# Half of the SiLU products split into float32r, one shared buffer pool, and an accumulating DMA in the rational stage

## The chip, the cores and the metric

One program on one core of a Trainium2 chip. The metric is the device time of one execution in microseconds. The engines named below are TensorE (PE in the profile, its weight loads PEld), VectorE (DVE), ScalarE (ACT), GpSimd (POOL) and the DMA queue of SyncE (SP). Each engine runs its own instructions strictly in the order in which the program lists them; semaphores make one engine wait for another.

## The reference

Three stages over 12480 tokens of 128 channels, all in float32; the second and third have 2048 hidden units.

```python
a2k = softmax(agents @ k.T / sqrt(128));  agent_v = a2k @ v      # 49 agents
x   = softmax(q @ agents.T / sqrt(128)) @ agent_v
h   = x @ moe_w_in;   x = (h * sigmoid(h)) @ moe_w_out           # SiLU
h   = x @ moe2_w_in                                              # rational function
P   = a[0] + a[1]*h + a[2]*h**2 + a[3]*h**3
Q   = 1 + abs(b[0])*abs(h) + abs(b[1])*h**2
out = (P / (Q + 1e-6)) @ moe2_w_out
```

The four weight matrices arrive as float64 and are turned into float32 on the chip.

## The kernel before

The tokens are cut into 25 groups: 24 of 512 tokens and one of 192. The 2048 hidden units are cut into 8 *pairs* of 2 x 128, so the work tile of one pair is 128 x 1024 float32 (4 KB in each partition). For each group, with p from 0 to 7:

- **M1** (lines 537, 538): 4 matmuls of pair p in float32r into a PSUM tile h; **S1** (line 544): ScalarE, s = Silu(h).
- **M2** (line 551): s times w_out in plain float32, summed over the pairs in the one PSUM bank x2. The profile lists each float32 matmul as two records, so a pair has 4.
- **XS** (lines 564, 565): VectorE splits x2 into a float32r high part xh and a rest xl.
- **M3** (lines 574 to 576): x2 times w2_in as three float32r products, low weights x xh, high weights x xl, high weights x xh: 6 matmuls for each pair, into a tile h.
- **U** (line 585 on VectorE for pairs 0 to 3, line 583 on ScalarE for pairs 4 to 7), **W1** (line 610), **W2** (line 614), both on VectorE: the cubic by Horner's rule without a[0], in a tile z.
- **AB** (line 592, ScalarE): m = |h|. **N** (line 598) and **Q** (line 606), both on GpSimd: y = (|b1| m + |b0|) m.
- **L** (line 619) and **R** (line 622), ScalarE, on two pairs at once (128 x 2048): 1/(1+y+1e-6) as sigmoid(-ln(y + 1e-6)).
- **G2** (line 626, VectorE): z = (z + a0) y. **M4** (line 635): z times w2_out in plain float32 into the PSUM bank ot. **O1** (line 647, ScalarE copy), **O2** (line 655, transposes), **O3** (line 661, ScalarE copy, and the store on SP).

Once for two groups the q stage makes the softmax weights of 1024 tokens: QT, QTc (line 459, ScalarE copy, which also issues the next q load on SP), QS, QV, QX, QM, QE, QN, QB, QBc (line 516, two ScalarE copies), QBl. Before the groups, k, v and the weights are loaded, the agents' attention is formed, and 16 jobs convert the weights: C0 to C2 on VectorE and ScalarE, C3 (line 756, GpSimd), and for w2_in also C4 (line 760, ScalarE) and C5 (line 764, GpSimd), which split it into float32r parts.

PSUM has three h tiles of two banks, one x2 and one ot bank. SBUF tiles come from rings of their own: 5 for s, 13 for z, 2 for m, 6 of 8 KB for y. The order of all instructions is written by a planner, `scheduled`, that plays the program through with a table of costs (`COST`), picks by priorities (`PLACE`), and emits the steps in its order. Silu, Ln, Sigmoid and Exp each need their own table on ScalarE, so the planner runs all L of a group, then all R, and S1 outside of that. Its first L of a group waits, in the plan, until `READY_Y` denominators are done (4 halves before, so all eight pairs).

Of the kernel before, what the change touches and what calls it, by code (L numbers as in the profile page):

```python
# [996 lines left out]
```

## Time and profile before

| | |
|---|---|
| three timed runs | 1263.23, 1265.34, 1265.42 us; median 1265.34 us |
| span of the profiled execution, first to last instruction | 1261.5 us, 3.8 us under that median |
| PE busy | 1235.0 us, 98% of the span |
| ACT busy | 1076.0 us, 85% |
| DVE busy | 1003.4 us, 80% |
| POOL busy | 764.2 us, 61% |
| DMA | HBM read 27.59 MB, most of it in the first 60 us |

The profiled execution is known by its span; what lies around the span is taken as the 3.8 us to the median. A busy PE is a PE with some matmul in it; the busy time alone doesn't say that it runs at its peak.

### The profile page before, as it was taken

The numbers are of one execution on the slowest core, as the hardware profiler recorded it, in microseconds if no ns is written. First come the engines' busy times: TensorE is split into PE (matmuls) and PEld (weight loads), VectorE is DVE, ScalarE is ACT, GpSimd is POOL, SyncE is SP. The second block draws the span as 40 slices with busy tenths as digits, with TensorE's granted clock in tenths as the row PEclk, the third lists the DMA queues.
The fourth block names the chain that finished last, engine by engine and source line by source line (L and its number), as shares of the span: only waits on it lengthen the run. The fifth ranks groups of instructions, "written<-read, shape, count | busy, mean of one in ns | idle before, by whom it ended". The sixth has DMA issues, their size and how long they took to land.

```text
span 1261.5 us, 12078 instructions
## 1 busy us (share of the span) xinstructions
PE 1235.0 (98%) x4393; PEld 740.7 (59%) x4393; DVE 1003.4 (80%) x960; ACT 1076.0 (85%) x997; POOL 764.2 (61%) x434
## 2 busy tenths in 40 slices
PE   9899899999999999999999999999999999999987
PEld 5656465556556556556566565565555565555654
DVE  4977887888868869869869869769769769769895
ACT  7677988988988988988988978978978979978896
POOL 2248667666566656656655755755755755755863
PEclk9999999999999999999999999999999999999999
DMA  9820000000000000000000000000000000000000
...
DMA packets 14675, 34.75 MB, mean 28 GB/s; under 512 B 1575, under 2 KB 5720, under 8 KB 14616
## 3 DMA queue, kind: packets, MB, share of 16 engines
...
q8 instruction: 35, 0.57, 0.2%
...
HBM read 27.59 MB, written 6.39 MB: 27 GB/s over the span
## 4 chain that ended last, share of the span: by engine, by line
PE 86%; DVE 6%; ACT 4%; DMA 2%; issue 1%; POOL 0%; SPq 0%; POOLq 0%; ACTq 0%; DVEq 0%
PE x L551 25%; PE ot L635 23%; PE h L537 7%; PE h L574 7%; PE h L538 7%; PE h L576 7%; PE h L575 7%; DVE z L610 2%; DVE z L614 1%; DVE z L585 1%; PE h L468 1%; PE h L451 1%; DMA kv<-in_k_dram 1%; PE ot L655 1%; DVE z L626 1%
## 5 line engine op out<-in xcount | busy, mean ns | idle before, releaser
L598 POOL TENSOR_SCALAR y<-m,bab 128x1024 f32<-128x1024 f32 (+1 forms) x200 | 265.4, 1329 | 409.8 <-ACT m L592 402.9
L606 POOL TENSOR_TENSOR y<-y,m 128x1024 f32<-128x1024 f32 (+1 forms) x200 | 469.0, 2357 | 7.5
L551 PE MATMUL x<-s,wo 128*128 128x512 f32 (+1 forms) x800 | 358.9, 584 | 3.1 <-ACT s L544 2.8
L635 PE MATMUL ot<-z,w2o 128*128 128x512 f32 x768 | 349.8, 596 | 6.8 <-DVE z L626 4.6
L610 DVE TENSOR_TENSOR z<-z,h 128x1024 f32<-128x1024 f32 (+1 forms) x200 | 237.8, 1191 | 141.2 <-ACT z L583 134.1
L626 DVE SCALAR_TENSOR_TENSOR z<-z,a_sb,y 128x1024 f32<-128x1024 f32 (+1 forms) x200 | 264.6, 1372 | 4.7 <-ACT y L622 4.7
L592 ACT ACTIVATE m<-h 128x1024 f32<-128x1024 f32 (+1 forms) x200 | 197.1, 1000 | 81.2 <-PE h L576 72.9
L614 DVE SCALAR_TENSOR_TENSOR z<-z,a_sb,h 128x1024 f32<-128x1024 f32 (+1 forms) x200 | 249.9, 1252 | 5.0 <-ACT m L592 0.5
L544 ACT ACTIVATE s<-h 128x1024 f32<-128x1024 f32 (+1 forms) x200 | 193.3, 1005 | 59.5 <-PE h L538 59.1
L635 PEld LDWEIGHTS ot<-z,w2o 128*128 128x128 f32 x768 | 143.6, 190 | 162.2 <-issue 145.1
L551 PEld LDWEIGHTS x<-s,wo 128*128 128x128 f32 x800 | 147.7, 190 | 138.5 <-issue 127.0
L574 PE MATMUL h<-xh,w2l 128*128 128x512 f32 (+1 forms) x400 | 190.9, 477 | 1.6 <-DVE z L614 1.2
L619 ACT ACTIVATE y<-y,eps 128x2048 f32<-128x2048 f32 (+1 forms) x100 | 191.4, 1957 | 0.8 <-POOL y L606 0.5
L537 PE MATMUL h<-xt,w1a 128*128 128x512 f32 (+1 forms) x400 | 185.9, 466 | 0.8 <-DVE z L614 0.7
L622 ACT ACTIVATE y<-y 128x2048 f32<-128x2048 f32 (+1 forms) x100 | 185.0, 1878 | 0.3
L576 PE MATMUL h<-xh,w2h 128*128 128x512 f32 (+1 forms) x400 | 155.9, 390 | 0.0
L575 PE MATMUL h<-xl,w2h 128*128 128x512 f32 (+1 forms) x400 | 155.3, 388 | 0.0
L538 PE MATMUL h<-xt,w1b 128*128 128x512 f32 (+1 forms) x400 | 155.1, 389 | 0.0
L585 DVE TENSOR_SCALAR z<-h,a_sb 128x1024 f32<-128x1024 f32 (+1 forms) x100 | 130.8, 1312 | 5.7 <-PE h L576 3.8
L583 ACT ACTIVATE z<-h,a_sb 128x1024 f32<-128x1024 f32 (+1 forms) x100 | 118.3, 1184 | 5.5 <-PE ot L635 3.5
L537 PEld LDWEIGHTS h<-xt,w1a 128*128 128x128 f32 x400 | 75.6, 189 | 44.1 <-issue 16.0
L574 PEld LDWEIGHTS h<-xh,w2l 128*128 128x128 f32 x400 | 75.9, 190 | 36.7 <-issue 20.0
...
## 6 DMA issues: line engine op xcount, KB each, us to landing
q<-in_q_dram SPq DMA_DIRECT2D x12, 512.0 KB, 3.3
out_dram<-ob SPq DMA_DIRECT2D x24, 256.0 KB, 2.0
raw<-in_moe_w_in_dram SPq DMA_DIRECT2D x8, 512.0 KB, 4.9
raw<-in_moe_w_out_dram SPq DMA_DIRECT2D x8, 512.0 KB, 7.5
s<-in_k_dram SPq DMA_DIRECT2D x7, 512.0 KB, 7.4
kv<-in_v_dram SPq DMA_DIRECT2D x7, 512.0 KB, 7.7
kv<-in_k_dram SPq DMA_DIRECT2D x5, 512.0 KB, 10.3
s<-in_v_dram SPq DMA_DIRECT2D x5, 512.0 KB, 8.0
```

What stands on the lines that cost most here:

```text
L537: nc.tensor.matmul(h[:, c, :w], w1a[:, f], xt, start=True, stop=False)
L538: nc.tensor.matmul(h[:, c, :w], w1b[:, f], xt, start=False, stop=True)
L551: nc.tensor.matmul(x2_t[i][:, : cols(i)], wo[:, 2 * p + c, :], s[:, c, : cols(i)], start=(p == 0 and c == 0), stop=(p == NP - 1 and c == 1),)
L574: nc.tensor.matmul(h[:, c, :w], w2l[:, f], xh_t[i], start=True, stop=False)
L575: nc.tensor.matmul(h[:, c, :w], w2h[:, f], xl_t[i], start=False, stop=False)
L576: nc.tensor.matmul(h[:, c, :w], w2h[:, f], xh_t[i], start=False, stop=True)
L598: nc.gpsimd.tensor_scalar(out=y_t[i, p // 2][:, p % 2], in0=m_t[i, p], scalar1=bab[:, 1:2], scalar2=bab[:, 0:1], op0=ALU.mult, op1=ALU.add,)
L606: eng.tensor_mul(out=y, in0=y, in1=m_t.pop((i, p)))
L610: nc.vector.tensor_mul(out=z, in0=z, in1=h)
L614: nc.vector.scalar_tensor_tensor(out=z, in0=z, scalar=a_sb[:, 1:2], in1=h, op0=ALU.add, op1=ALU.mult)
L626: nc.vector.scalar_tensor_tensor(out=z, in0=z, scalar=a_sb[:, 0:1], in1=r, op0=ALU.add, op1=ALU.mult)
L635: nc.tensor.matmul(ot_t[i][:, : cols(i)], w2o[:, 2 * p + c, :], z[:, c, :], start=(p == 0 and c == 0), stop=(p == NP - 1 and c == 1),)
```

## The change

1. **M2 split for half of the pairs.** Pairs 2, 3, 6 and 7 (`SPLIT = [1, 3]`) get what M3 has: SH (VectorE copy of s to float32r), SL (GpSimd subtraction; in group 0 VectorE for pairs 2 and 6), then six float32r matmuls. Pairs 0, 1, 4, 5 stay as they are. Two more weight jobs need C4 and C5.
2. **The rational stage is rescaled.** A once-run step CF (33 small VectorE instructions on 128 x 1 columns, 2 on ScalarE) forms coefficients, so that x2 can be multiplied by |b0| in XS, and the denominator becomes 1 + |h| + kap h². SQ (ScalarE, Square with a per-partition scale) gives kap h² for all 8 pairs; W1 becomes a scalar_tensor_tensor of h and that square; U, N and Q are gone.
3. **|h| is added by DMA.** Y issues, on GpSimd's queue, an SBUF to SBUF DMA of 512 KB with accumulation, m into y. L and R now work on one pair each.
4. **Copies moved.** QTc, QBc, O1 and O3 go from ScalarE to VectorE.
5. **One pool of 34 slots of 4 KB** for s, sh, sl, xh/xl, y, m, z, q, qT and the output tiles, in place of the rings. q loads (LQ) and stores (OD) are steps of their own on SP's queue. The loads have a new order, and group 0 no longer waits for all weight jobs before AB.
6. The planner's costs and priorities are new; `READY_Y` is 8.

The core of the diff:

```diff
-U_ACT = (4, 5, 6, 7)
-NZ = 13
-NY = 6
-NM = 2
-NS = 5
+SPLIT = [1, 3]
+HIGH = 'DDDDDDDD'
+LOW = "PPPPPPPP"
+LOW_0 = "DPDPDPDP"
+POLY = 'SSSSSSSS'
+ABS = "AAAAAAAA"
+MAG = 'GGGGGGGG'
+COPY = 'DDDD'
+NF = 34
...
+    def SH(i, p, slot):
+        sh = t_f(slot, F32R)
...
+            (eng.dma_start if HIGH[p] == "G" else eng.tensor_copy)(sh[:, :, :w], s_t[i, p][:, :, :w])
+    def SL(i, p, slot):
...
+        eng = nc.gpsimd if (LOW if i else LOW_0)[p] == "P" else nc.vector
+        eng.tensor_sub(
+            out=sl[:, :, :w], in0=s_t.pop((i, p))[:, :, :w], in1=sh_t[i, p][:, :, :w].bitcast(F32)
+        )
...
+            if p // 2 in SPLIT:
...
+                nc.tensor.matmul(x2, low, sh, start=start, stop=False)
+                nc.tensor.matmul(x2, high, sl, start=False, stop=False)
+                nc.tensor.matmul(x2, high, sh, start=False, stop=stop)
...
+        nc.vector.tensor_scalar_mul(out=xh, in0=ps[:, :w], scalar1=B0)
+        nc.vector.scalar_tensor_tensor(
+            out=xl, in0=ps[:, :w], scalar=B0, in1=xh.bitcast(F32), op0=ALU.mult, op1=ALU.subtract
+        )
...
+    def SQ(i, p, slot):
+        y = part_of(y_t, i, p, slot)
+        nc.scalar.activation(y, h2_t[i, p][:, :, : cols(i)], AF.Square, scale=ROOT)
...
+            nc.vector.scalar_tensor_tensor(
+                out=part_of(z_t, i, p, slot), in0=h, scalar=COEF[2], in1=y_t[i, p],
+                op0=ALU.mult, op1=ALU.add,
+            )
...
+    def Y(i, p, slot=None):
+        m = m_t.pop((i, p))
+        y = y_t[i, p]
+        if MAG[p] == "G":
+            nc.gpsimd.dma_start(out=y, in_=m, accum_op=ALU.add)
...
+    def L(i, p):
+        nc.scalar.activation(y_t[i, p], y_t[i, p], AF.Ln, bias=eps)
+    def R(i, p):
+        nc.scalar.activation(y_t[i, p], y_t[i, p], AF.Sigmoid, scale=-1.0)
...
+                done = sum((done_y(h), g, h) in end for h in range(8))
                 if batch is None and (p or done < READY_Y):
                     return None
```

## Rows read from the trace of the kernel before

**Rows 1.** Busy time by stretch: us; PE, PEld, DVE, ACT, POOL; clock; DMA share; GB/s

```profile
20.00:40.00 20.00, 16.98 (x103) 9.70 (x103) 14.41 (x29) 17.20 (x35) 3.65 (x3) 0.91 0.96 350
60.00:200.00 140.00, 131.84 (x435) 78.07 (x436) 114.83 (x123) 114.98 (x114) 89.43 (x51) 0.99 0.08 25
608.35:704.17 95.82, 95.82 (x318) 56.76 (x317) 76.11 (x68) 83.62 (x73) 58.71 (x32) 1.00 0.03 11
1150.00:1261.50 111.50, 99.55 (x380) 62.28 (x378) 87.91 (x90) 90.17 (x91) 69.64 (x43) 0.98 0.03 11
```

**Rows 2.** Waits, 608.35 to 704.17 us: who waited for whom, us, times, longest

```profile
ACT m L592 <- PE h L576: 7.2, 6, 3.8
...
ACT s L544 <- PE h L538: 4.2, 4, 1.8
```

**Rows 3.** Timeline of PE: start, us, line, tiles, count

```profile
620.55 3.60 PE L551 MATMUL x<-s,wo 128*128 128x512 f32 x8
623.98 0.60 PE L655 MATMUL ot<-ident,oT 128*128 128x128 f32 x4
...
632.34 0.40 PE L574 MATMUL h<-xh,w2l 128*128 128x512 f32 x1
...
635.14 0.40 PE L537 MATMUL h<-xt,w1a 128*128 128x512 f32 x1
```

**Rows 4.** Timeline of ACT

```profile
606.52 1.19 ACT L583 ACTIVATE z<-h,a_sb 128x1024 f32<-128x1024 f32 x1
607.61 1.01 ACT L592 ACTIVATE m<-h 128x1024 f32<-128x1024 f32 x1
608.51 2.00 ACT L619 ACTIVATE y<-y,eps 128x2048 f32<-128x2048 f32 x1
...
621.94 0.58 ACT L647 COPY oT<-ot 128x512 f32<-128x512 f32 x1
622.41 3.73 ACT L622 ACTIVATE y<-y 128x2048 f32<-128x2048 f32 x2
```

**Rows 5.** Groups by line and shape, whole span, ACT: busy us, mean ns

```profile
L619 ACT ACTIVATE y<-y,eps 128x2048 f32<-128x2048 f32 x96 | 187.9, 2000 | 0.3
...
L622 ACT ACTIVATE y<-y 128x2048 f32<-128x2048 f32 x96 | 181.9, 1922 | 0.3
...
L619 ACT ACTIVATE y<-y,eps 128x768 f32<-128x768 f32 x4 | 3.5, 928 | 0.5 <-POOL y L606 0.5
L622 ACT ACTIVATE y<-y 128x768 f32<-128x768 f32 x4 | 3.2, 835 | 0.0
```

**Rows 6.** Groups by line and shape, 608.35 to 704.17 us, DVE

```profile
L610 DVE TENSOR_TENSOR z<-z,h 128x1024 f32<-128x1024 f32 x17 | 20.7, 1218 | 15.0 <-ACT z L583 14.9
L614 DVE SCALAR_TENSOR_TENSOR z<-z,a_sb,h 128x1024 f32<-128x1024 f32 x16 | 20.5, 1279 | 0.4
L585 DVE TENSOR_SCALAR z<-h,a_sb 128x1024 f32<-128x1024 f32 x8 | 10.7, 1338 | 0.0
```

**Rows 7.** The same, POOL

```profile
L606 POOL TENSOR_TENSOR y<-y,m 128x1024 f32<-128x1024 f32 x16 | 38.0, 2386 | 0.7
```

**Rows 8.** Timeline of DVE and POOL, weight jobs beside each other

```profile
72.39 0.42 DVE L719 TENSOR_SCALAR ma<-raw 128x512 uint32<-128x512 uint32 x1
72.72 1.52 DVE L723 TENSOR_SCALAR ec<-ex 128x512 f32<-128x512 uint32 x1
...
72.55 1.41 POOL L764 TENSOR_TENSOR w2l<-w,w2h 128x512 fp32r<-128x512 f32 x1 [0.73 <-ACT w2h L760]
```

**Rows 9.** DMA issues: KB each, median us from issue to landing

```profile
q<-in_q_dram SPq DMA_DIRECT2D x12, 512.0 KB, 3.3
out_dram<-ob SPq DMA_DIRECT2D x24, 256.0 KB, 2.0
```

**Rows 10.** Timeline of DVE, two instructions on 128 x 1 columns

```profile
58.01 0.14 DVE L910 TENSOR_SCALAR rs<-ot 128x1 f32<-128x1 f32 x1
58.19 0.16 DVE L911 RECIPROCAL rs<-rs 128x1 f32<-128x1 f32 x1
```

More of the change, by code (lines that the diff above doesn't have):

```diff
@@ L171, in group_steps, with then @@
         stage(2, [("C1", job, 0)], [], [("w", job), ("cb", job)])
-        split = job // 4 == 2
+        split = job // 4 == 2 or job - 4 in SPLIT
         after = [("C2", job, 0)] + [("KS", batches - 1, 0)] * (job >= 12)
-        stage(3, after, [("w2", ("w2", job))] * split, [("cb", job)])
+        stage(3, after, [], [("cb", job)])
         if split:
-            stage(4, [("C3", job, 0)], [], [("w2", job)])
-            stage(5, [("C4", job, 0)], [], [("w2", job)])
-    conv += [("V2", n, 0) for n in range(4)]
+            stage(4, [("C3", job, 0)], [], [("cb", job)])
+            stage(5, [("C4", job, 0)], [], [("cb", job)])
+    add("CF", 0, 0, [("V2", 3, 0)], at=-3 + PLACE["CF"][0])
+    conv += [("V2", n, 0) for n in range(4)] + [("QX", 0, 0)]
+    conv = conv[:-5]
+    attended = [("V2", n, 0) for n in range(4)] + [("QX", 0, 0)]
+    near = NKV + NRAW + NCA + NCB
+    group_steps.freed = [
+        (range(NKV), [("AV", batches - 1, 0)]), (range(NKV, near), conv), (range(near, NF), attended),
+    ]
+    def then(name, g, p):
+        return [(name, g - (p == 0), (p - 1) % pairs)] * (g + p > 0)
     for g in range(groups):
@@ L188, in group_steps @@
+            add("M2", g, p, [after] + [("M2", g, ORDER[at - 1])] * (at > 0) + first, x2, [("x2", g)] + uses, cost=cost)
+        add("XS", g, 0, [("M2", g, p) for p in range(pairs)] + [("CF", 0, 0)] * (g == 0), [("f", ("xh", g))], [("x2", g)])
         for p in range(pairs):
-            h, z, m, y = ("h2", g, p), ("z", g, p), ("m", g, p), ("y", g, p // 2)
+            h, z, y = ("h2", g, p), ("z", g, p), ("y", g, p)
             first = [("C5", 8 + p // 2, 0)] if g == 0 else []
-            add("M3", g, p, [("XS", g, 0)] + first, [("h", h)], [("xh", g)])
@@ L206, in group_steps @@
-        add("O1", g, 0, [("M4", g, p) for p in range(pairs)], [("oT", ("oT", g))], [("ot", g)])
-        add("O2", g, 0, [("O1", g, 0)], [("ot", ("o2", g))], [("oT", g)])
-        add("O3", g, 0, [("O2", g, 0)], [("ob", ("ob", g))], [("o2", g)])
+            z, y = ("z", g, p), ("y", g, p)
+            add("G2", g, p, [("R", g, p), ("W2", g, p)], [], [z, y])
+            first = [("C3", 12 + p // 2, 0)] if g == 0 else []
+            add("M4", g, p, first + [("G2", g, p)] + [("M4", g, p - 1)] * (p > 0), [("x2" if g + 1 == groups else "ot", ("ot", g))] if p == 0 else [], [z, ("ot", g)])
@@ L209, in group_steps @@
+        add("O1", g, 0, [("M4", g, p) for p in range(pairs)], [("f", ("o", g))], [("ot", g)])
+        add("O2", g, 0, [("O1", g, 0)], [("ot", ("o2", g))], [("o", g)])
+        add("O3", g, 0, [("O2", g, 0)], [], [("o2", g), ("o", g)])
+        add("OD", g, 0, [("O3", g, 0)], [], [("o", g)])
     for b in range(batches):
-        chain = ("QT", "QTc", "QS", "QV", "QX", "QM", "QE", "QN", "QB", "QBc", "QBl")
+        chain = ("LQ",) * (b > 0) + ("QT", "QTc", "QS", "QV", "QX", "QM", "QE", "QN", "QB", "QBc", "QBl")
@@ L221, in group_steps @@
             add(
-                name, b, 0, [(chain[i - 1], b, 0)] if i else [("M1", 2 * b - 2, 0)] if b else [land["q", 0]], [takes[name]] if name in takes else [],
+                name, b, 0, [(chain[i - 1], b, 0)] if i else [("M1", 2 * b - 2, 0)] if b else [land["q", 0]], [takes[name]] if name in takes and (b or name != "QTc") else [],
                 uses.get(name, []), at=(2 * b if b else -2) + PLACE[name][0],
@@ L241, in scheduled @@
     free = {tag: [0.0] * n for tag, n in bufs.items()}
+    free["f"] = [None] * NF
+    held_by = [(slots, set(steps), steps) for slots, steps in group_steps.freed]
     taken = {tag: 0 for tag in bufs}
@@ L282, in may_start @@
                     return None
-                done = sum(all(("Q", g, 2 * h + i) in end for i in (0, 1)) for h in range(4))
+                done = sum((done_y(h), g, h) in end for h in range(8))
                 if batch is None and (p or done < READY_Y):
@@ L336, in scheduled @@
                 n_sig[g] = n_sig.get(g, 0) + 1
-                batch = None if n_sig[g] == 4 else batch
+                batch = None if n_sig[g] == 8 else batch
+        for slots, left, steps in held_by:
+            if k in left:
+                left.remove(k)
+                if not left:
+                    for i in slots:
+                        free["f"][i] = max(end[x] for x in steps)
         out.append((name, g, p, slot))
@@ L746, in attention_silu_rational_kernel @@
     w2_t = {}
+    turn = [-1, -1]
     def conv_out(job):
```

375 lines of the change are left out of this document (240 added, 135 removed), and 69 rows, old and new, of tables (COST, PLACE).

## The prediction

> **What bounds the kernel now.** I read the busy time by stretch first. The q stage runs once for two groups, so the pattern repeats every two groups, and the stretch from 608.35 to 704.17 us is one such repeat: 95.82 us, in which PE is busy for 95.82, ACT for 83.62, DVE for 76.11 and POOL for 58.71 us [rows 1]. A busy PE need not be a fast one, so the timeline of PE must show that matmuls follow each other without a gap: the matmuls below do, and the clock is at the upper of its two levels, 2.4 GHz, in that stretch. PE bounds the steady part, and what is taken off PE there shortens the run as long as no other engine takes over. PE is idle in two other places: 140.00 - 131.84 = 8.2 us between 60 and 200 us, where the pipeline fills, and 111.50 - 99.55 = 12.0 us after 1150 us, where it drains [rows 1].
>
> The waits say how ACT, the next busiest, spends its 12.2 us of idle time in a repeat: 7.2 us before AB and 4.2 us before S1, waiting for matmuls [rows 2]. ACT is ahead of PE, and these 11.4 us are the cover that the change draws on.
>
> **The change part by part**, per repeat of two groups.
>
> *PE.* Eight float32 records of M2 start at 620.55 and the next instruction at 623.98: 3.43 us for two pairs, 1.715 us for one. Twelve float32r matmuls start at 632.34 and the next instruction at 635.14: 2.80 us for two pairs, 1.40 for one [rows 3]. A split M2 pair is the same six matmuls as an M3 pair with the same operand shapes, so it saves 0.315 us. Four pairs in 24 full groups are 96 pairs: 30.2 us. The group of 192 tokens I count at 0.1. One repeat becomes 95.8 - 8 x 0.315 = 93.3 us of PE work. This hangs on sh and sl being there in time: SH and SL together take about 3 us behind S1, and M2 of the whole pairs and M3, M4 of other groups stand in between.
>
> *ACT loses:* a U from 606.52 to 607.61 is a step of 1.09 us, an AB from there to 608.51 one of 0.90, and a duration is about 0.10 longer than its step. O1 from 621.94 to 622.41 is 0.47 [rows 4]. L of 2048 columns takes 2.00, R 1.92 [rows 5], steps 1.90 and 1.82. Eight U are 8.7, eight L 15.2, eight R 14.6, four copies O1 and O3 1.9, QTc 0.9 (an AB's size), two QBc copies 0.9: 42.2 us.
>
> *ACT gains:* sixteen L and R of 1024 columns. A line through 768 columns (0.93 and 0.84) and 2048 columns [rows 5] gives 1.14 and 1.05, steps 1.04 and 0.95: 16.6 and 15.2. SQ is not in the trace; it lies between AB (no per-partition operand, 0.90) and U (two, 1.09), I take 1.00: 16.0, bounds 14.4 and 17.4. Sum 47.8 (46.2 to 49.2). Net +5.6 (4.0 to 7.0): ACT 89.2 us (87.6 to 90.6) of PE's 93.3. It fits, with 4.1 us of cover in place of 12.2.
>
> *DVE.* It loses eight U of 1.25 (1.338 less the overlap), 10.0 us. W1 changes from 1.218 to the kind of W2, 1.279: 16 x 0.06 = 1.0 [rows 6]. QTc (1.2), two QBc and four O1/O3 copies (0.6 each, half of 1.2) add 4.8. Eight SH: a 512-column SBUF to SBUF instruction takes 0.42 us, its successor starting 0.33 later, so 1024 columns at that rate are 0.60, and at the rate of W2 1.2: 4.8 to 9.6, I take 4.8 since it is the same kind of one-input SBUF instruction. Net +0.6 (to 5.4): 76.7 to 81.5 of 93.3 us. Not the bound.
>
> *POOL* loses all N and Q, its whole 58.7 us, and gains eight SL at 2.39, 19.1 us [rows 7], and 16 DMA issues whose price no row shows; up to 2 us each they would still leave it at 51. Queued behind each issue on POOL are the next SL and Y: a Y waits there for AB and W1, and an SL behind it makes M2 of its pair late. Cover: two or more whole pairs of M2 or other groups' matmuls. SL and SH share one thing: L723 takes 1.52 in place of 0.42 us beside a POOL instruction of 1.41 [rows 8], so an SH that meets an SL stands for up to 2.4 us. Eight such meetings would be 19 us, DVE then at 96: this is the far end for DVE. The planner's `PORT` set is to keep SH and SL apart, but it holds only as well as the planned times do: the pair in the rows is in that set too. I count a meeting in few of them, and no cost, since DVE then still has over 10 us to spare.
>
> *DMA.* 16 accumulating transfers of 512 KB. A plain load of 512 KB lands in 3.3 us, a store of 256 KB in 2.0, so 256 KB more cost 1.3; an accumulation also reads its destination, 512 KB more: 3.3 to 5.9 us to land [rows 9], against 1.2 + 2.4 us of N and Q before. The engines: 350 GB/s at a share of 0.96 [rows 1] is 1.44 us for 512 KB, twice that if both operands count: 16 x 2.9 = 46 of 93 us. It fits; it would bind at 5.8 us each. SP's queue carries three transfers in a repeat and is nearly empty: LQ and OD cost nothing; a q load that stands behind a store has a whole repeat to land in.
>
> *Start and end.* CF's 33 VectorE instructions at 0.18 us [rows 10] are 6 us on a chain ahead of XS of group 0; four SH and two SL there add 5; two more C4 and C5 are small. PE had other groups' M1 and M2 to do then, so I charge 2 us (0 if that covers it, 8 if PE's idle time there doubles). The later stretches gain by a free POOL, and lose by the landing time: 0, bounds -6 (half the idle time of the drain) and +4.
>
> *Sum.* 1265.3 (span 1261.5 and 3.8 around it) - 30.3 + 2, and 1 us for small stalls of PE now that ACT is at 96%: **1238 us**.
>
> **The rivals.**
>
> *ACT takes part of it.* ACT waited for PE because the order and three h tiles made it wait, not because it had nothing to do. If half of the 11.4 us stays, a repeat is 89.2 + 5.7 = 94.9 us, only 0.9 less than now, and twelve repeats give 11: 1265.3 - 11 + 3 = 1257. For it: the waits are few and long, up to 3.8 us [rows 2], so they stand at places where the order puts ACT behind PE. Against it: waits shrink by themselves where the waiting engine becomes later. Between 1246 and 1264.
>
> *Y lands late (slower).* L of a group stands in ACT's order; if its y has not landed, ACT stands, and all behind it, S1 first, then M2 and PE. With w us of such waits in each group a repeat takes 89.2 + 2w, and it decides from 2w = 6.6, w = 3.3 us. At w = 5 it is 99.2: 12 x 3.4 = 41 us more, 1308. For it: a landing of up to 5.9 us, an issue that can stand behind an SL, two transfers in flight that halve each other. Against: by the plan the first L comes only when all eight Y are through, so only y of the last pairs can be late, and seven L (7 us) run ahead of the last.
>
> *VectorE holds up the issues.* A VectorE and a GpSimd instruction on SBUF can exclude each other for the whole instruction [rows 8]. If an SH (0.6 us) does that to the issue of a DMA on GpSimd, eight of them hold Y back by 4.8 us in a repeat; all of it passed on to ACT gives 89.2 + 4.8 = 94.0, 1.8 less than now: 1265.3 - 22 + 3 = 1246, the edge of the first rival, with which it shares its chance. The Trainium skill, "SBUF — State Buffer", section SBUF: two separate sides, states such a lock, and with it speaks against this change: VectorE's float32 copy from SBUF to SBUF, which SH is, keeps GpSimd from writing the descriptors of a DMA that it issues. No row here shows such a DMA.
>
> *More than the sum.* The fill and the drain, 20 us of PE idle, close by a third: about 1225.
>
> *The split saves nothing.* If six weight loads instead of four held PE back, an M2 pair would stay at 1.7 us and only the costs were left: 1267. Against it stands M3, which runs with the same six weight loads at 1.40 [rows 3].
>
> **How the numbers follow.** The forecast has 0.57, its own range 1228 to 1246; ACT taking part, or VectorE holding up the issues, 0.18; Y late 0.18; more than the sum 0.03; no saving 0.04. The time is that of the forecast, 1238. The range of 8 in 10 takes in the forecast and most of the ACT case: 1228 to 1262. About 0.2% (2.5 us) is what a measurement of this kernel can tell from no change. Faster by more than that: 0.57 + 0.16 + 0.03 = 0.76. Within it: 0.02 of the ACT case and 0.03 of no saving: 0.05. Slower: 0.18 + 0.01 = 0.19.
>
> **What the profile after would show.** Right: a repeat of about 93.3 us with PE busy throughout; the split lines of M2 at 0.23 us from start to start; ACT near 89 us of it, DVE 77 to 82, POOL far below before; AB and S1 waiting for PE less than 11.4 us. Wrong: PE idle in the steady stretch, with ScalarE's s as releaser (the ACT case), or ACT idle before L with the DMA of y as releaser (Y late); a landing of that DMA above 6 us; SH near 1.2 or 3 us; a start in which XS of group 0 comes late and PE stands.

## The result, and the profile of the changed kernel

The changed kernel takes **1251.84 us** (median of 4 runs, 1249.23 to 1253.01), the kernel before 1265.17 us beside it (4 runs): ratio 0.9896, 95% interval 0.9882 to 0.9911, some 13 us faster. The forecast was 1238 us. The time lies in the range of 8 in 10 (1228 to 1262), and outside the forecast's own (1228 to 1246).

Busy time by stretch of the changed kernel, with the columns of [rows 1]; the third line is one repeat of two groups, from XS of group 13 to XS of group 15 (groups count from 0):

```profile
20.00:40.00 20.00, 14.52 (x88) 7.28 (x84) 17.79 (x30) 14.01 (x25) 5.98 (x5) 1.00 0.85 313
60.00:200.00 140.00, 124.94 (x508) 81.47 (x507) 119.10 (x166) 111.64 (x125) 56.69 (x38) 0.96 0.41 92
701.30:794.50 93.20, 92.93 (x333) 59.39 (x332) 76.63 (x75) 88.12 (x90) 33.62 (x24) 1.00 0.51 102
1150.00:1251.20 101.20, 91.62 (x366) 58.32 (x364) 72.26 (x85) 83.55 (x105) 30.81 (x26) 0.98 0.45 84
```

This repeat takes 93.2 us, the shortest of them. Over seven repeats, from XS of group 8 to XS of group 22 (467.65 to 1122.9 us; 459.73 to 1130.0 us in the kernel before), one takes 93.6 us where 95.75 were needed before and 93.3 were forecast. PE is busy for 92.9 of the 93.2 us; ACT has 88.1 us (forecast 89.2), DVE 76.6 (76.7 to 81.5), POOL 33.6 (at most 51). The second line is what went wrong: PE idles 15.1 us between 60 and 200 us where it idled 8.2 [rows 1], at a lower mean clock, while DVE's busy time rose from 114.8 [rows 1] to 119.1.

The same by stages shows where the 10.3 us between the two spans come from (the profiled execution of the changed kernel, 1253.01 us, is the longest of its four). First the kernel before, then the changed one (same columns):

```profile
0.00:80.00 80.00, 71.69 (x507) 48.37 (x508) 58.05 (x115) 56.94 (x101) 22.83 (x27) 0.98 0.77 279
80.00:200.00 120.00, 114.42 (x381) 67.71 (x380) 97.82 (x91) 99.41 (x92) 81.84 (x46) 0.99 0.03 12
200.00:400.00 200.00, 199.37 (x661) 118.44 (x660) 165.68 (x145) 174.92 (x154) 127.27 (x67) 1.00 0.03 11
400.00:1150.00 750.00, 750.00 (x2470) 443.89 (x2469) 593.91 (x522) 654.53 (x563) 462.61 (x254) 1.00 0.03 10
```

```profile
0.00:80.00 80.00, 61.97 (x472) 41.88 (x473) 64.63 (x130) 50.28 (x95) 27.14 (x31) 0.95 0.71 264
80.00:200.00 120.00, 111.20 (x402) 72.29 (x402) 100.97 (x120) 101.29 (x108) 48.41 (x32) 0.96 0.42 87
200.00:400.00 200.00, 199.23 (x707) 126.80 (x705) 168.41 (x161) 193.57 (x196) 72.49 (x53) 1.00 0.55 108
400.00:1150.00 750.00, 746.16 (x2651) 475.03 (x2650) 608.13 (x592) 707.50 (x713) 269.45 (x192) 1.00 0.51 101
```

Length less PE's busy time is PE's idle time. It grows by 9.7 us up to 80 us, 3.2 up to 200, 0.1 up to 400 and 3.8 up to 1150 us, and falls by 2.4 in the drain (12.0 [rows 1] to 9.6): together +14.6. PE's busy time falls by 24.9 us, and 24.9 - 14.6 is the 10.3 by which the span is shorter. The clock column adds to it. PE is granted 1.2 GHz from 41.5 to 48.4, from 79.1 to 82.5 and from 120.0 to 126.9 us, each time from within a wait; in the kernel before this is so from 36.5 to 39.9 and from 155.9 to 159.4 us. That is 10.3 us more at half the clock up to 200 us, worth at most 5.1 us. So between 25 and 30 us of PE's work were saved (30.3 forecast), and the start takes 13 to 18 of them back.

Groups by line and shape of the changed kernel (busy us, mean ns), and two kinds of DMA (KB, median us to land):

```profile
L742 ACT ACTIVATE f<-f,eps 128x1024 f32<-128x1024 f32 x192 | 204.1, 1138 | 0.9 <-DMA f<-f 0.7
L745 ACT ACTIVATE f<-f 128x1024 f32<-128x1024 f32 x192 | 190.3, 1064 | 0.3
L687 ACT ACTIVATE f<-h,cf 128x1024 f32<-128x1024 f32 x192 | 213.9, 1114 | 14.9 <-PE h L530 13.0 <-PE x L658 1.1 <-POOL f L638 0.4
L631 DVE CAST f<-f 128x1024 fp32r<-128x1024 f32 x96 | 83.0, 884 | 4.8 <-ACT f L621 4.8
L638 POOL TENSOR_TENSOR f<-f,f 128x1024 fp32r<-128x1024 f32 x94 | 245.1, 2613 | 205.1 <-DVE f L631 175.8 <-PE h L615 22.3 <-POOL f L638 5.5
L728 POOL DMA_DIRECT2D f<-f x200 | 176.8, 896 | 506.2 <-DVE f L701 388.7 <-issue 116.0 <-DVE qmx L565 1.0
```

```profile
f<-f POOLq DMA_DIRECT2D x192, 512.0 KB, 4.7
out_dram<-f SPq DMA_DIRECT2D x24, 256.0 KB, 2.0
```

L takes 1.14, R 1.06 and SQ 1.11 us (1.14, 1.05, and a step of 1.00, which is a duration of 1.10). The accumulating DMA costs GpSimd 0.90 us and lands in 4.7 (3.3 to 5.9), and ScalarE waited for it 0.7 us in all before L (L742).

A split pair of M2 among its neighbours, timeline of PE:

```profile
736.76 0.39 PE L653 MATMUL x<-f,wol 128*128 128x512 f32 x1
736.98 0.40 PE L654 MATMUL x<-f,woh 128*128 128x512 f32 x1
737.22 0.40 PE L655 MATMUL x<-f,woh 128*128 128x512 f32 x1
...
738.14 3.59 PE L658 MATMUL x<-f,wof 128*128 128x512 f32 x8
```

Its six matmuls take 738.14 - 736.76 = 1.38 us, against 1.40 in M3 and 1.715 whole [rows 3].

The chain at the first SiLU, timelines of DVE, POOL, ACT and PE of the changed kernel, and the same place on PE in the kernel before:

```profile
75.33 1.28 DVE L991 TENSOR_SCALAR cf<-cf 128x2 f32<-128x2 f32 x1
76.64 0.23 DVE L985 TENSOR_TENSOR cf<-cf 128x1 f32<-128x1 f32 x2
```

```profile
75.30 1.29 POOL L885 TENSOR_TENSOR f<-f 128x512 f32<-128x512 f32 x1
```

```profile
74.19 0.21 ACT L994 ACTIVATE cf<-b_sb 128x2 f32<-128x2 f32 x1
76.96 0.21 ACT L1009 ACTIVATE cf<-a_sb 128x4 f32<-128x4 f32 x1 [2.56 <-issue]
77.18 1.28 ACT L621 ACT_TABLE_LOAD   x1
78.47 1.94 ACT L621 ACTIVATE f<-h 128x1024 f32<-128x1024 f32 x2
```

```profile
76.59 0.39 PE L615 MATMUL h<-xt,w1b 128*128 128x512 f32 x1
79.55 3.43 PE L658 MATMUL x<-f,wof 128*128 128x512 f32 x4 [2.58 <-ACT f L621]
82.34 0.86 PE L614 MATMUL h<-xt,w1a 128*128 128x512 f32 x1
```

```profile
69.54 1.98 PE L551 MATMUL x<-s,wo 128*128 128x512 f32 x4 [0.92 <-ACT s L544]
```

CF's second Abs on ScalarE (L1009) overwrites columns that VectorE's first CF instructions read. The last of these ends at 76.87 us, and it starts at 76.96; the profile names no releaser, so that it waited for them is read from the program. It stands 2.56 us, and the table load and S1 of the first two pairs are queued behind it. 1.1 of these 2.56 us are no work of CF: L991 takes 1.28 us beside a GpSimd instruction of 1.29 us, and 0.17 in start_all, where GpSimd is idle beside it. PE has filled all three h tiles by then, has nothing else, and stands 2.58 us, 0.92 us in the kernel before; the four records that follow take 3.43 us at the lower clock instead of 1.88 in cf_none below.

### The profile page after: what moved, and what is told of

Same layout as the page of the kernel before. It is cut to its first block, busy times and chain, and to the rows that moved or that the text cites. A ratio compares the mean times of both kernels' runs of the same rounds, so it can differ in the third digit from the quotient of the medians.

```text
span 1251.2 us, 13128 instructions
## 1 busy us (share of the span) xinstructions
PE 1210.2 (97%) x4593; PEld 774.3 (62%) x4593; DVE 1014.4 (81%) x1083; ACT 1136.2 (91%) x1212; POOL 448.3 (36%) x334
## 4 chain that ended last, share of the span: by engine, by line
PE 79%; ACT 10%; DVE 5%; issue 3%; DMA 2%; POOL 0%; ACTq 0%; DVEq 0%; POOLq 0%; SPq 0%
PE ot L758 20%; PE x L658 12%; PE h L614 7%; PE h L677 6%; PE h L679 6%; PE h L678 6%; PE h L615 6%; PE x L653 3%; PE x L655 3%; PE x L654 3%; ACT f L745 3%; DVE f L701 1%; ACT f L687 1%; ACT L621 1%; DMA f<-f 1%
## 5 line engine op out<-in xcount | busy, mean ns | idle before, releaser
L701 DVE SCALAR_TENSOR_TENSOR f<-h,cf,f 128x1024 f32<-128x1024 f32 (+1 forms) x200 | 248.3, 1253 | 170.8 <-ACT f L687 98.4
L758 PE MATMUL ot<-f,w2o 128*128 128x512 f32 x768 | 353.8, 597 | 2.2 <-DVE f L787 1.3
L638 POOL TENSOR_TENSOR f<-f,f 128x1024 fp32r<-128x1024 f32 (+1 forms) x98 | 249.1, 2547 | 219.9 <-DVE f L631 190.6
L749 DVE SCALAR_TENSOR_TENSOR f<-f,cf,f 128x1024 f32<-128x1024 f32 (+1 forms) x200 | 246.9, 1262 | 3.8 <-ACT f L745 3.8
L737 DVE SCALAR_TENSOR_TENSOR f<-f,cf,h 128x1024 f32<-128x1024 f32 (+1 forms) x200 | 247.2, 1249 | 1.8
L711 ACT ACTIVATE f<-h 128x1024 f32<-128x1024 f32 (+1 forms) x200 | 199.9, 999 | 37.2 <-PE h L679 31.2
L687 ACT ACTIVATE f<-h,cf 128x1024 f32<-128x1024 f32 (+1 forms) x200 | 218.4, 1093 | 14.9 <-PE h L530 13.0
L742 ACT ACTIVATE f<-f,eps 128x1024 f32<-128x1024 f32 (+1 forms) x200 | 208.5, 1117 | 2.2 <-DMA f<-f 1.9
L621 ACT ACTIVATE f<-h 128x1024 f32<-128x1024 f32 (+1 forms) x200 | 184.4, 1012 | 12.7 <-PE h L615 11.6
L745 ACT ACTIVATE f<-f 128x1024 f32<-128x1024 f32 (+1 forms) x200 | 193.7, 1041 | 0.3
L678 PE MATMUL h<-f,w2h 128*128 128x512 f32 (+1 forms) x400 | 154.9, 387 | 0.6 <-DVE f L666 0.5
L679 PE MATMUL h<-f,w2h 128*128 128x512 f32 (+1 forms) x400 | 155.1, 388 | 0.0
```

What stands on the lines that cost most here:

```text
L638: eng.tensor_sub(out=sl[:, :, :w], in0=s_t.pop((i, p))[:, :, :w], in1=sh_t[i, p][:, :, :w].bitcast(F32))
L679: nc.tensor.matmul(h[:, c, :w], w2h[:, f], xh_t[i], start=False, stop=True)
L687: nc.scalar.activation(y, h2_t[i, p][:, :, : cols(i)], AF.Square, scale=ROOT)
L701: nc.vector.scalar_tensor_tensor(out=part_of(z_t, i, p, slot), in0=h, scalar=COEF[2], in1=y_t[i, p], op0=ALU.mult, op1=ALU.add,)
L737: nc.vector.scalar_tensor_tensor(out=z, in0=z, scalar=COEF[1], in1=h, op0=ALU.add, op1=ALU.mult)
L745: nc.scalar.activation(y_t[i, p], y_t[i, p], AF.Sigmoid, scale=-1.0)
```

## The experiments

Times are medians. X2 is the start of the maximum of the key stage, M1 that of the first M1, XS0 and XS1 those of XS of groups 0 and 1, in the traces.

| kernel | us | ratio to before, 95% | X2 | M1 | XS0 | XS1 |
|---|---|---|---|---|---|---|
| before | 1265.17 | 1 | 35.1 | 64.9 | 92.7 | 127.4 |
| changed | 1251.84 | 0.9896 (0.9882, 0.9911) | 42.4 | 72.8 | 103.6 | 143.6 |
| m2_whole | 1272.92 | 1.0061 (1.0048, 1.0074) | 42.2 | 72.7 | 104.6 | 145.1 |
| no_gy | 1247.91 | 0.9863 (0.9849, 0.9876) | 41.8 | 71.9 | 102.5 | 142.4 |
| cf_none | 1250.47 | 0.9879 (0.9863, 0.9895) | 43.5 | 74.4 | 101.9 | 142.2 |
| cf_early | 1250.40 | 0.9890 (0.9875, 0.9905) | 46.2 | 76.8 | 104.4 | 144.4 |
| ec_act | 1252.24 | 0.9895 (0.9880, 0.9911) | 42.3 | 73.0 | 103.6 | 143.6 |
| loads_v | 1251.87 | 0.9891 (0.9877, 0.9904) | 41.8 | 72.3 | 103.1 | 143.2 |
| loads_ec | 1252.24 | 0.9890 (0.9873, 0.9906) | 42.0 | 72.7 | 103.7 | 144.3 |
| start_all | 1255.40 | 0.9924 (0.9911, 0.9936) | 41.7 | 79.1 | 106.7 | 146.2 |
| k_first | 1258.39 | 0.9942 (0.9928, 0.9955) | 40.6 | 80.3 | 110.9 | 150.3 |
| w2o_late | 1256.80 | 0.9930 (0.9918, 0.9943) | 43.2 | 73.4 | 104.0 | 148.1 |
| w2o_out | 1248.99 | 0.9876 (0.9859, 0.9892) | 41.5 | 71.5 | 100.7 | 138.5 |
| conv_out4 | 1249.89 | 0.9874 (0.9858, 0.9891) | 45.1 | 74.0 | 101.7 | 142.0 |
| raw7 | 1251.97 | 0.9897 (0.9884, 0.9910) | 43.1 | 73.5 | 104.1 | 144.1 |
| raw7_ec | 1251.82 | 0.9897 (0.9884, 0.9910) | 42.4 | 73.1 | 103.7 | 143.2 |
| raw7_cf | 1250.76 | 0.9889 (0.9876, 0.9901) | 45.2 | 75.1 | 102.6 | 142.1 |
| raw7_cf_ec | 1253.20 | 0.9912 (0.9897, 0.9928) | 44.8 | 75.4 | 103.0 | 142.4 |
| conv_none | 1243.75 | 0.9820 (0.9801, 0.9838) | 40.0 | 69.3 | 95.3 | 133.6 |
| conv_none_k | 1239.69 | 0.9797 (0.9783, 0.9810) | 39.3 | 69.1 | 95.1 | 132.0 |

In all of them the planned order is that of the changed kernel, apart from the steps named. The intervals are some 2 us to each side. The stages are read from one trace for each kernel. Ten of the kernels (the changed one, m2_whole, no_gy, cf_none, ec_act, loads_v, loads_ec, start_all, w2o_late, w2o_out) have the same steps on PE, VectorE, ScalarE and GpSimd ahead of X2, and yet it lies between 41.5 and 43.5 us, so a difference of less than 2 us in X2 says little.

**The parts whose price was disputed.** m2_whole:

```diff
-                high, low = woh[:, at : at + P], wol[:, at : at + P]
-                sh, sl = sh_t[i, p][:, c, :w], sl_t[i, p][:, c, :w]
-                nc.tensor.matmul(x2, low, sh, start=start, stop=False)
-                nc.tensor.matmul(x2, high, sl, start=False, stop=False)
-                nc.tensor.matmul(x2, high, sh, start=False, stop=stop)
+                sh = sh_t[i, p][:, c, :w].bitcast(F32)
+                nc.tensor.matmul(x2, wof[:, at : at + P], sh, start=start, stop=stop)
```

> The changed kernel with the four split pairs of M2 taken as one plain float32 product of the rounded high part, as two records each, instead of three float32r products (96 full pairs; the low part of SiLU is still formed but not multiplied, which leaves the correction terms out). SH, SL, the parts of the weights and all else stay. Theory, TensorE bounds the repeat and the saving in products reaches the end in full: 0.315 us more for each of 96 pairs, 30 us, 1282 (1278 to 1285), a repeat of two groups 95.8 to 96.1 us. Rival, another engine already bounds the repeat of the changed kernel (ScalarE 95% busy): the end moves by less than 15 us, under 1267.

It is 21 us slower than the changed kernel, between the theory and the rival. One of its repeats, and the stage from 400 to 1150 us:

```profile
475.50:571.00 95.50, 95.50 (x317) 56.84 (x316) 76.77 (x75) 89.13 (x90) 33.58 (x25) 1.00 0.50 99
400.00:1150.00 750.00, 749.43 (x2482) 445.69 (x2481) 595.17 (x580) 697.15 (x697) 265.73 (x188) 1.00 0.50 98
```

Over the same seven repeats (475.53 to 1142.6 us) one takes 95.3 us, 1.7 more than the 93.6 of the changed kernel, and twelve times 1.7 are 20 of the 21 us. So PE bounds the repeat, and the product's price reaches the end there. The size was 21 and not 30, since a repeat differs by 1.7 us instead of 2.5. Some 0.4 us of that are idle time: PE idles 750.00 - 749.43 = 0.6 us between 400 and 1150 us where the changed kernel idles 3.8. The other 0.4 us have no cause shown. PE's waits of the changed kernel in that stretch name ScalarE's SiLU:

```profile
PE h L614 <- ACT f L621: 3.8, 9, 1.0
```

Its start is as late as that of the changed kernel, though M2 is whole: what the start loses comes neither from the three products nor from a PE that has become faster. no_gy:

```diff
-            nc.gpsimd.dma_start(out=y, in_=m, accum_op=ALU.add)
+            pass
```

> The changed kernel without the 200 accumulating transfers (the |h| that they add to the denominator is left out; AB still forms it; SQ, L, R and all else stay). Theory, the transfers are hidden: steady repeat 93.5 us as now, the end within 2 us, 1250 to 1253. Rival, Y lands late or VectorE keeps GpSimd from issuing: PE's idle time between 400 and 1150 us (3.8 us) goes and the end comes 4 us or more earlier, 1248 or less. Second rival, the start and the drain wait for them: the repeat unchanged, but the last group's way from M3 to its end some 2 to 4 us shorter.

The repeat stays 93.6 us over the seven, and PE idles 4.0 us from 400 to 1150 us (3.8 with the transfers): in the steady part they are hidden, as the theory had it. The end is some 4 us earlier, though, at the edge of the intervals. Of the 5.8 us between the two spans the trace has 2.0 by XS of group 22 (0.6 already at X2, which no transfer of this kind precedes) and 3.8 behind it, in the drain. Part of these 3.8 is the clock: in the changed kernel PE is granted 1.2 GHz from 1191.8 to 1195.2 us, in no_gy not. The way from XS of group 22 to the end takes 127.8 to 128.3 us in seven of the kernels of the table with one such stretch there (cf_none, ec_act, k_first, w2o_late, w2o_out, conv_out4, raw7_cf; 128.3 in the changed one), 126.1 to 126.6 us in seven without one ahead of the last instructions (cf_early, loads_v, loads_ec, start_all, raw7, raw7_ec, raw7_cf_ec), and 124.5 in no_gy. So some 2 us are left to the transfers: the second rival is nearer there.

**One step of the start at a time.** cf_none replaces CF by `nc.vector.memset(cf, 0.5)`; cf_early moves it:

```diff
+    nc.sync.dma_start(out=a_sb, in_=ca.partition_broadcast(P))
+    nc.sync.dma_start(out=b_sb, in_=cb.partition_broadcast(P))
...
+    CF(0)
     late = None
     for name, g, p, slot in scheduled(NG, NP, REST / GW):
```

The two loads stand behind that of the agents and no longer in the step LD.

> The changed kernel with the coefficient step CF replaced by one memset of cf to 0.5 on VectorE (the 33 VectorE instructions and the two ScalarE Abs are left out, so the rational function has other coefficients; everything after it runs as before). Theory, VectorE and ScalarE queue at the start: CF holds VectorE for 7.6 us (75.3 to 83.0 in the trace of the changed kernel) and keeps the first SiLU behind Abs, so PE stands for 2.58 us ahead of the first M2 and then runs some 3.4 us at half clock; without CF the first M2 comes about 4 us earlier and the whole ends 4 to 8 us earlier, 1244 to 1248. Rival, the start hangs on transfers and on the key stage alone and CF lies beside that: 1250 to 1253. Rival, the 7.6 us are only lent (VectorE catches up in the steady part, where it has 19% of its time free, and PE has other work): under 2 us, 1250 to 1252.

> The changed kernel with the loads of the rational coefficients put right behind the load of the agents, and the whole of CF emitted ahead of the first planned step instead of behind the second M1; nothing is left out. VectorE is busy for 10.6 of its first 20 us, so CF's 7.6 us should fit there. Theory, CF in its place delays the start: as much as leaving it out brings, less 1 to 2 us for the first conversions that it holds up: 1245 to 1249. Rival, transfers and key stage set the start: 1250 to 1254, later if the first conversion of weights is held up by CF.

From M1 to XS0 both need 27.5 and 27.6 us instead of 30.8, so CF in its place does cost 3.3 us there, and PE idles 3.7 instead of 6.3 us from 60 to 80. But cf_early delays VectorE's first conversions and with them X2 by 3.8 us, and the end of neither differs from the changed kernel's by more than the intervals. The theory's 4 to 8 us fell. ec_act:

```diff
-        nc.vector.tensor_copy(eT[:n, :m, :], ps)
+        nc.scalar.copy(eT[:n, :m, :], ps)
```

> The changed kernel with the 13 copies of the transposed agent weights (EC, PSUM to SBUF, 128 x 512) on ScalarE instead of VectorE; nothing is left out. VectorE is busy 18.1 of 20 us in both windows from 40 to 80 us, ScalarE 12.1 and 10.4. The copies take 8.3 us on VectorE. Theory, VectorE is what bounds the start: the first M1 comes 4 to 8 us earlier (72.8 now) and the kernel ends 3 to 8 us earlier, 1244 to 1249. Rival, the start hangs on the last key and value transfers (last v lands at 64.8 us): first M1 within 1 us of 72.8, 1250 to 1253. Other side: the copies stand behind the Exp of the next block on ScalarE and the chain Exp, transpose, copy, product gets longer: 1254 to 1258.

M1 and the time are unchanged, although 8.3 us leave VectorE: the copies are not what bounds X2 to M1. loads_v:

```diff
-        what = LOADS[i]
+        what = (LOADS[:24] + "3;vvvvv7vvv5vv:" + LOADS[39:])[i]
```

> The changed kernel with the same transfers in another order on SP's queue: behind the 24th load it issues five blocks of v, one weight, three v, two weights, two v and so on instead of letting the third and the fifth weight of that stretch stand ahead of the v blocks; all else, the order on the other engines too, stays. Theory, the queue: in the trace of the changed kernel SP stands from 29.5 to 39.8 and from 42.3 to 52.6 us for a raw buffer that VectorE's join of an earlier weight (L867) frees, with the v blocks behind; the last v lands at 64.8 (58.3 before) and the first M1 starts at 72.8 (64.9 before). With v ahead the last v lands at 57 to 60, the first M1 starts at 66 to 69, the whole ends 3 to 7 us earlier: 1245 to 1249. Rival, VectorE sets the start (18.1 of 20 us busy from 40 to 80 us): v lands early, yet the first M1 stays at 71 to 73, and the time at 1250 to 1253. Other side: a weight comes later and its conversion stops VectorE: 1254 and more.

The last v is issued at 50.4 instead of 55.5 us, M1 stays: the rival's outcome. loads_ec is both edits; start_all adds CF behind the 35th transfer:

> The kernel loads_v with the 13 EC copies on ScalarE as in ec_act; nothing is left out. Theory, first the transfers, behind them VectorE: each cover hides the other, so that together they bring more than the first alone: first M1 2 to 4 us ahead of that of loads_v, 1242 to 1247. Rival, transfers alone: as loads_v within 1 us.

> The kernel loads_ec with CF emitted behind the 35th transfer, where VectorE and ScalarE wait, instead of behind the second M1; nothing is left out. In cf_none and cf_early the way from the first M1 to XS of group 0 was 27.5 us instead of 30.8. Theory: those 3.3 us add to what loads_ec brings, 1239 to 1245. Rival, PE has M1 of later groups to do in their place, and the way to the later XS takes the time back: as loads_ec within 1 us.

loads_ec is the same again. In start_all VectorE stands 3.12 us ahead of CF, since CF's Abs is queued on ScalarE behind Exp and copies, and then CF stands in front of a join; M1 comes 6 us later. Taken out of its place, CF finds no free one. k_first:

```diff
-        what = LOADS[i]
+        what = (LOADS[:13] + "kkkkvqk86vv" + LOADS[24:])[i]
```

Besides, C0 to C3 of jobs 6 and 8 and C4 and C5 of job 8 go from ahead of X2 to places behind QN, EX 3, EX 5, EC 1, EC 2 and EX 9.

> The changed kernel with two weights (blocks 4 and 2 of w2_in and w_out: jobs 8 and 6) loaded behind the last block of k instead of ahead of it, and their conversion (C0 to C5) moved behind the maximum step X2 instead of among the KM ahead of it; nothing is left out. In the trace of before 4 weights stand ahead of the last k and X2 comes at 36.7 us; in that of after 7 do, and it comes at 42.4. Theory, the key stage waits for k and for the conversions ahead of KM: X2 comes 3 to 5 us earlier (37 to 40), and the first M1 with it, if nothing else holds it: 69 to 71 and 1247 to 1249. Rival, the same conversions hold VectorE up later instead (it is 90% busy from 40 to 80 us): X2 earlier, the first M1 still at 72 to 74, 1250 to 1253.

(The 36.7 us in this text is where the second Exp of before stands; its X2 is at 35.1.) X2 comes 1.8 us earlier and M1 7.5 us later: PE waits 8.0 us for the copies EC, which VectorE now does behind conversions. The 7 us of this work are not free behind X2 either.

w2o_out skips C0 to C3 of jobs 12 to 15; w2o_late moves those of 14 and 15 to behind W2 of the fifth pair:

> The changed kernel with the conversion of the four w2_out blocks left out (C0 to C3 of jobs 12 to 15 on VectorE, ScalarE and GpSimd; the transfers stay, and M4 multiplies by what the key stage left in that buffer). Theory, group 0: these jobs stand among W1 and W2 of group 0 on VectorE (106 to 121 us), M1 waits for h tiles for 1.67 and 2.42 us at 117 to 122 us and then runs at 1.2 GHz from 120.0 to 126.9: without them XS of group 1 comes 5 to 8 us earlier than 143.6 and the end 4 to 8 us earlier, 1244 to 1248. Rival, the order: PE's idle time moves to the next wait, for L's and R's of group 0 on ScalarE, and the end moves less than 2 us, 1250 to 1253.

> The changed kernel with the conversion of the last two w2_out blocks (jobs 14 and 15) moved from among W1 and W2 of the first three pairs of group 0 to behind W2 of its fifth pair, where VectorE stands for 3.47 us at 125.1 us; nothing is left out. w2o_out, which left four such jobs out, ended 5.2 us earlier in its span and gave XS of group 1 at 138.5 instead of 143.6. Theory, VectorE's place in the order: half to all of this, XS of group 1 at 139 to 141 and 1246.5 to 1249.5. Rival, the total of VectorE's work up to 135 us: XS of group 1 stays at 143 to 144, 1250 to 1253.

Left out, these jobs give XS1 5.1 us earlier. The median is 2.9 us lower, though, which the intervals don't tell from none, and misses the theory's range; the span of 1246.0 us (1251.2) is that of the shortest of four executions beside the longest of four. PE's waits from 100 to 150 us in the changed kernel:

```profile
PE h L614 <- DVE f L737: 4.1, 2, 2.4
```

W2 (L737) stands behind those conversions on VectorE, and M1 waits for its h tile. With these jobs left out it is 2.4 us. Moved, they do not give the time back: in w2o_late the same wait is 2.4 too, but a new one stands beside it,

```profile
PE h L614 <- ACT f L621: 2.7, 1, 2.7
```

and XS1 comes 4.5 us later. The moved C1 stand among the SiLU on ScalarE there, and on VectorE one join takes 1.76 and one SH 2.80 us instead of 0.69, both beside a GpSimd instruction. conv_out4 skips C0 to C5 of jobs 6, 8, 10 and 11:

> The changed kernel with the conversion of four weight blocks left out (jobs 6, 8, 10 and 11: one of w_out, three of w2_in; C0 to C5 on VectorE, ScalarE and GpSimd; their places are filled with zeros by GpSimd at the start, the transfers stay). Up to the first M1 VectorE is busy for about 13 us more than in the kernel before: 12 jobs stand there instead of 10, each longer. Theory, VectorE's and ScalarE's conversion work sets the start: without 12 to 14 us of it on VectorE the first M1 comes 5 to 9 us earlier (64 to 68) and the end 4 to 8 us earlier, 1244 to 1248. Rival, k and v and the chain Exp, transpose, copy, product set it: first M1 at 71 to 73, 1249 to 1252.

Its reading is spoilt: the fill on GpSimd, from 3.5 to 7.9 us, delays agT and X2 (45.1). From X2 to XS0 it needs 56.6 us instead of 61.2. raw7 gives three transfers buffers of their own:

```diff
-        t = t_f(NKV + len(raw_t) % NRAW, I64, [P, CW])
+        at = len(raw_t)
+        t = (pool.tile([P, CW], I64, tag=f"more{at % 7}", name="more", bufs=1)
+             if at in (4, 5, 6, 11) else t_f(NKV + at % NRAW, I64, [P, CW]))
```

> The changed kernel with three more raw weight buffers (12 KB per partition in the space of the first stage) for the fifth, sixth, seventh and twelfth weight transfers; order and all else stay. In the trace of the changed kernel SP stands from 11.3 to 16.2 and from 18.5 to 22.3 us for a raw buffer that VectorE's join frees, with blocks of k behind; the last k is issued at 26 us instead of 22. Theory, the queue and its buffers: SP doesn't stand, the last k is issued at 18 to 22 us, X2 comes at 37 to 40, the first M1 4 to 6 us earlier, 1245 to 1249. Rival, the conversions on VectorE and ScalarE ahead of KM hold X2: k lands early, X2 stays at 41 to 43, 1249 to 1253.

> raw7 with the 13 EC copies on ScalarE. Theory, causes hide each other: once k and v are early, VectorE's 8.3 us of EC bound the way from X2 to the first M1 (30.4 us now, 28.3 before): 2 us less than raw7 at the first M1 and at the end. Rival, that way is the chain of Exp on ScalarE and the products, which EC on ScalarE only lengthens: as raw7 or 1 to 2 us later.

> raw7 with CF emitted ahead of the first planned step and its two loads in front, as in cf_early. In cf_early the way from the first M1 to XS of group 0 fell from 30.8 to 27.6 us, but the first M1 came 4.0 us later, with SP standing until 21 us for a raw buffer. Theory: with buffers free CF early costs nothing ahead of X2, and 3 us more come off than in raw7: 1242 to 1246. Rival, CF delays VectorE's first conversions and all behind them: first M1 3 to 4 us later than in raw7, the end as raw7 within 1 us.

> raw7 with both, CF early and EC on ScalarE. Theory, the start is a set of bounds that lie close to each other, so that only taking several away together shows: 1240 to 1245. Rival, another bound of the start (the order of M1 to M3 of the first three groups) gives it back: 1248 to 1252 as most runs so far.

In raw7 SP stands for VectorE's joins for 0.7 us up to 60 us instead of 25, but the last k is issued at 25.1 us (25.8), not at 18 to 22, and X2 is where it was. The transfer engines are busy for a share of 0.91 and 0.99 of the first two stretches of 20 us (0.91 and 0.85 in the changed kernel): with free buffers an early issue waits there. The theory of the queue and its buffers fell; the three others lie within the intervals as well. CF early brings its 3 us from M1 to XS0 and gives X2 at 45.2 us even with free buffers.

**All of it together.** conv_none leaves out CF and the conversion of eight blocks, conv_none_k loads two of them behind k besides:

```diff
-        if name in ("GS", "GY"):
+        if name in ("GS", "GY") or (name in ("C0", "C1", "C2", "C3", "C4", "C5") and g in (6, 8, 10, 11, 12, 13, 14, 15)):
             continue
```

Both also have CF's memset of cf_none and let M2 and M3 read converted blocks in place of those left out; conv_none_k has the line of `LOADS` of k_first besides.

> The changed kernel without the conversion of eight of its sixteen weight blocks (jobs 6, 8, 10, 11 and 12 to 15, C0 to C5 on VectorE, ScalarE and GpSimd) and without CF (one memset): M2 and M3 read other blocks in their place, M4 what the key stage left; the transfers stay, and no fill on GpSimd stands at the start as it did in conv_out4. Theory, conversion work on VectorE sets the start: some 30 us less of it give a first M1 at 68 to 71, XS of group 1 at 133 to 137 instead of 143.6, and an end 8 to 13 us earlier, 1239 to 1244. Rival, the order and the landing of k hold the first M1 at 72 to 73 and the removals do not add up: 1246 to 1250, what w2o_out gave alone.

> conv_none with two weight transfers behind the last block of k instead of ahead of it, as in k_first, but with no conversion to be moved behind X2. A block takes 1.3 us on the transfer engines, which are full until 30 us. Theory, the bytes ahead of k: X2 2.5 to 3.5 us earlier than in conv_none, the first M1 with it, the end 2 to 4 us earlier: 1236 to 1242. Rival, X2 hangs on the KC, KS and KM of each block and not on its landing: within 1 us of conv_none.

1243.75 and 1239.69 us: 8 and 12 us off, the second within 2 us of the forecast. conv_none's theory holds in M1, XS1 and the time; conv_none_k's holds in the time, but its X2 is 0.6 us earlier and not 2.5 to 3.5. conv_none_k by stage:

```profile
0.00:80.00 80.00, 69.39 (x501) 47.41 (x502) 52.67 (x95) 49.19 (x87) 21.55 (x26) 0.96 0.75 279
80.00:200.00 120.00, 112.37 (x414) 72.67 (x413) 93.86 (x92) 104.21 (x106) 42.68 (x30) 1.00 0.46 90
```

PE's idle time up to 80 us falls from 18.0 to 10.6 (8.3 before), and the 1.2 GHz stretches behind 80 us are gone; VectorE has 52.7 us of work up to 80 us instead of 64.6. From X2 to M1 it still takes 29.8 us, as in before (29.8): that way is not what the conversions lengthen. They act ahead of X2, and from M1 to XS1 (62.9 us instead of 70.8). That the order of the transfers brought the 4 us between the two is not shown: X2 has 0.6 of them, and the clock differs. Behind 80 us conv_none's profiled execution has four stretches of 3.4 us at 1.2 GHz ahead of its last instructions, conv_none_k's none. The shortest of conv_none's five executions, at a mean granted clock of 0.997, took 1239.21 us, as long as the four of conv_none_k at 0.997 (1238.45 to 1240.97); the others, at 0.991 to 0.995, took 1242.40 to 1244.98.

## Why the forecast was right and wrong

**Right: the bound, and what it is worth.** PE bounds the repeat before and after; a split pair costs what an M3 pair costs, and a repeat keeps 2.1 of the 2.5 us; ACT, DVE and POOL have in the repeat what was worked out to within 1.1 us, POOL less than its upper bound. ScalarE's cover of 4 us held nearly: its waits for matmuls shrank from 11.4 us [rows 2] to these,

```profile
ACT f L711 <- PE h L679: 2.4, 2, 2.1
ACT f L687 <- PE h L530: 1.7, 1, 1.7
```

and PE waits for it 0.5 us in a repeat. "ACT takes part of it" would have a repeat of 94.9, "Y lands late" idle time before L; neither is there. The time does lie in the region of the first of them, and so in the range of 8 in 10 that was made to take it in, but for another reason: that is luck.

**Slightly off: small stalls.** 1 us was charged for PE's small stalls; 3.8 are there between 400 and 1150 us, 0.6 with M2 whole: this is ScalarE's part, at a third of a per cent of the time. That an SH meets an SL in few cases and at no cost held too: 8 of 75 stood for it, as the last section shows.

**Wrong: "Start and end".** The step that failed reads "PE had other groups' M1 and M2 to do then, so I charge 2 us (0 if that covers it, 8 if PE's idle time there doubles)". Measured: 12.9 us more idle time up to 200 us, and up to 5 us of clock. It failed in three ways. At the place of CF PE had no other work: the three h tiles were full and S1 stood behind CF's Abs. The sum counted CF, SH and SL, but not what the new order and COPY put on VectorE ahead of the first M1. Up to there VectorE is busy for 45.84 of 64.9 us in the kernel before and 58.09 of 72.8 us in the changed one, 12.3 us more: twelve C0 instead of eleven, eleven joins (C2) instead of nine, QTc and QBc, and instructions that take longer. First before, then after (lines grouped up to the first M1):

```profile
L741 DVE SCALAR_TENSOR_TENSOR sb<-raw,sb 128x512 uint32<-128x512 uint32 x9 | 6.2, 684 | 0.0
L719 DVE TENSOR_SCALAR ma<-raw 128x512 uint32<-128x512 uint32 x10 | 5.3, 526 | 0.0
```

```profile
L867 DVE SCALAR_TENSOR_TENSOR f<-f,f 128x512 uint32<-128x512 uint32 x11 | 10.7, 977 | 0.0
L844 DVE TENSOR_SCALAR f<-f 128x512 uint32<-128x512 uint32 x12 | 8.3, 688 | 0.0
```

Three of the eleven L867 took 1.76 us and three of the twelve L844 1.50 us, and each of these six began 0.1 to 0.5 us behind the start of a GpSimd instruction of 1.3 to 1.7 us; the other L867 took 0.68 to 0.69 us, the other L844 0.41 to 0.43. So the conversions became longer by standing beside GpSimd. Ahead of X2 five such instructions are longer than the shortest of their kind by 4.2 us in all, in the kernel before one by 0.5 us.

All 12.3 us, these 4 among them, lie ahead of X2: there VectorE is busy for 30.2 us instead of 17.9, and from X2 to M1 for 27.9 us in both kernels. The last maximum of the key stage (KM) shows what that does. First the last product on PE and its KM in the kernel before, then the same in the changed kernel with what stands ahead of it:

```profile
32.58 0.39 PE L834 MATMUL ot<-w2o,agT 128*64 128x96 f32 x4
33.37 0.26 DVE L842 TENSOR_REDUCE mxs<-ot 128x1 f32<-128x96 f32 x1 [0.32 <-ACT sT L839]
```

```profile
37.31 0.39 PE L968 MATMUL ot<-w2o,agT 128*64 128x96 f32 x4
37.46 0.69 DVE L864 SCALAR_TENSOR_TENSOR f<-f,f 128x512 f32<-128x512 uint32 x1
37.62 1.65 POOL L885 TENSOR_TENSOR wof<-f 128x512 f32<-128x512 f32 x1 [7.88 <-DVE f L867]
38.06 1.76 DVE L867 SCALAR_TENSOR_TENSOR f<-f,f 128x512 uint32<-128x512 uint32 x1
39.74 0.68 DVE L976 TENSOR_REDUCE mxs<-x 128x1 f32<-128x512 f32 x1
41.41 0.25 DVE L976 TENSOR_REDUCE mxs<-ot 128x1 f32<-128x96 f32 x1
```

The KM starts 0.40 us behind the end of its product in the kernel before and 3.71 us behind it in the changed one, since VectorE is still at joins, at the KM before and at QM; it starts 3.71 us behind it in all ten kernels that are alike up to X2, and 2.30 us in conv_none and conv_none_k. So 3.3 us of the 7.3 by which X2 is late are VectorE's queue. The rest is the product itself, which ends 4.7 us later (37.70 instead of 32.97 us), less 0.7 us that the way from this KM to X2 is shorter.

And a late start does not stay where it is: the three stretches at 1.2 GHz begin in PE's waits of 3.19 us (up to 42.0 us), 2.58 us (up to 79.55) and 2.42 us (up to 122.2), and PE loses in them again. What is shown: CF and eight conversions are worth 8 us of the end, CF 3.3 us of the way from M1 to XS0; w2_out's four alone give XS1 5.1 us earlier and nothing at the end that is clear of the intervals. The kernel before has to convert the same sixteen blocks; it is their place, beside CF, the copies and GpSimd, in the changed order that costs, and no other place that was tried is cheaper. What stays open is which part of the 4.7 us is the bytes ahead of the last k (seven weights instead of four) and which the work ahead of the earlier products: the last product ends at 36.6 us in conv_none and at 36.1 in conv_none_k, against 36.8 to 38.9 in the ten.

**The drain** was charged with 0 (-6 to +4) and gave -2.4 of idle time.
